# Opening order, bias engine, loops in the overflow path and the decoding rhythm of a fused attention, expert layer and feed-forward kernel

## The chip, the cores and the metric

The kernel runs on one core of a Trainium2 chip. The metric is the time of one execution in microseconds of device time; the median of several executions is compared. The engines are TensorE (PE, with its weight loads as PEld), VectorE (DVE), ScalarE (ACT), GpSimd (POOL) and SyncE (SP, which here issues most transfers). Each runs its own list of instructions in order and waits on semaphores for the others.

## The reference

Three layers follow each other, all in float32. Attention: 2 batches of 8 heads, 576 tokens, 64 wide, with rotary positions on q and k, a softmax over keys, and the product with v. The result is a matrix of 1152 tokens by 512. Expert layer: `logits = x @ w_gate + modality_bias[modality_id]`, each token goes to the expert with the largest logit out of 8, and the output is `gate * (relu(x @ w1[e]) @ w2[e])`, 512 to 1024 to 512. Feed-forward: `h = x @ w_in` (512 to 2048), `g = h * tanh(softplus(h))`, `g @ w_out` (2048 to 512).

With the inputs measured here every batch uses two experts, with 283 to 293 tokens each.

## The kernel before, in words

Products keep float32 accuracy by splitting an operand into a high part (`fp32r`, a rounded copy) and a low part (the rest); a product is then two or three matmuls. So every stage has splits: ACT or POOL write the high part, DVE or POOL subtract to get the low part.

**Attention** (about the first 175 us). For each head, prep loads q and k (`p_load`, `xs`), multiplies by the rotary tables (`p_mul`, L824), adds (`p_add`, L828), makes the high part (`p_hi`, L834) and the low part (`p_lo`, L843) in a buffer `ab` of which there is one, and then four transfers restack it into `sq` and `sk` (`p_stack`, L852 to L855). Scores (L877), maximum (L887), exp (L894), transposes (L907), their splits (L927, L933) and the product with v (L948) follow. Head 0 is prepared by hand in `p_first`, from L789. The order of all other attention work is written by a planner, `Plan`: each operation has an engine, an estimated duration, a key (its rank) and dependencies, and the planner walks a model clock. The estimates are only used to choose the order; the chip then runs it in that order. The planner starts from times at which each engine is supposed to come free (L1008) and from done times of the hand-written part (L1015). Two side jobs are planned too: `setup_dma`, which writes zeros into the padding rows of a scratch tensor in DRAM (two transfers, L277), and `setup_bias`, which makes each token's modality bias (nine small operations on DVE, L286 to L298).

**Expert layer** (to about 312 us). Tokens are sorted by expert in scratch; a tile is 304 rows of one expert. Each batch has two main tiles, (0,0), (0,1), (1,0), (1,1), run by `moe_tile`, with the expert's weights in 8 chunks of 512 KB, each split into high and low by ACT and POOL (L586, L591). An expert with more rows, or a third expert, gives extra tiles. They run in a loop on the device (L1274) between tiles (0,1) and (1,0). Its count is read from memory and is zero for these inputs: the engines come to the loop, meet, and branch past its body. That body is a whole `moe_tile`, written out: by the code 12 transposes, 96 matmuls of the first layer and 96 of the second.

**Feed-forward** (to the end). Weights come as 64-bit words and are decoded by three integer operations per chunk on DVE (`dec`, L1189, L1194, L1199; 16 chunks, 48 operations). Some are done during the expert layer; the rest run beside the feed-forward. There, step q of 32 takes one chunk: q below 16 for the first 640 rows, then again for the other 512. A step has two units `(q, i)`; each has 12 matmuls `h_unit` (L1349), three ACT passes, a DVE reciprocal and a fused multiply (L1371, L1372), a split on ACT and POOL (L1383, L1389), and the matmuls `o_unit` (L1406). The order is a list of events with times in units (`at2`): step q stands at 2q. A unit's matmuls need the PSUM buffer that the DVE multiply of three units before gives back. The weight split of a step, `split_w` (L1332 on ACT, L1333 on POOL), stands at 2q - 1.5. The decoding stands where it must be done in time for that:

```
for z in range(3):
    at2(m - 4.05 + 0.6 * z, lambda n=3 * q + z + 1: decode(n - nd[0]))
```

It is a catch-up: the operation is only issued if fewer than `n` have been.

Of the kernel before, what the change touches and what calls it, by code (L numbers as in the profile page):

```python
# [10 lines left out]
F32 = mybir.dt.float32  # L11
# [3 lines left out]
ALU = mybir.AluOpType  # L15
# [23 lines left out]
P = {'sd': (3,), 'dl': (10, 20), 'qd': (2, 3), 'alt': (0.1, 4), 'd0': 41, 'vl': 9, 'c': (-145.0, 22.5, -2.0), 'w3': 3, 'rq': (0.45, 0.47, 0.2), 'dec': (8, 8, 8), 'rl': 3, 'ah': 0, 'eps': 0.05, 'slack': 0.1}  # L39
# [171 lines left out]
def moe_kernel(ctx: ExitStack, tc: tile.TileContext, aps, out):  # L211
# [63 lines left out]
    def setup_dma():  # L275
        for r0 in (0, T + NTOK):
            nc.sync.dma_start(  # L277
                out=scratch[r0:r0 + T].rearrange("(p a) (h c) -> p (a h) c", p=16, h=2),
                in_=zero[:16, None, :].to_broadcast([16, T // 8, RW // 2]),
            )  # L280

    def setup_bias():
        m = kp.tile([128, B, 5], F32, name="mf")
        sel = kp.tile([128, 2, B, 5], F32, name="msel")
        tmp = kp.tile([128, B, 5, NE], F32, name="mtmp")
        nc.vector.tensor_copy(m, mod[:, :, :, 0])  # L286
        for v in range(2):
            nc.vector.tensor_scalar(
                out=sel[:, v], in0=m, scalar1=float(v), scalar2=None, op0=ALU.is_equal
            )  # L290
        for b in range(B):
            sh = [128, 5, NE]
            for v, o in ((0, lbias), (1, tmp)):
                nc.vector.tensor_tensor(
                    out=o[:, b], in0=sel[:, v, b, :, None].to_broadcast(sh),
                    in1=mbias[:, None, v].to_broadcast(sh), op=ALU.mult,
                )
            nc.vector.tensor_tensor(out=lbias[:, b], in0=lbias[:, b], in1=tmp[:, b], op=ALU.add)  # L298
# [438 lines left out]


    def attention(actx, hook):
# [49 lines left out]
        def p_first():  # L789

            V = nc.vector
            x = xin.pop(0)
            sq = p2.tile([128, S], F32R, tag="sq", name="sq0", bufs=3)
            sk = p2.tile([128, 2, S], F32R, tag="sk", name="sk0", bufs=3)
            for c in (slice(0, NC2), slice(NC2, S)):
                V.tensor_tensor(out=x[:, :, c], in0=x[:, :, c], in1=tabs[:, :, c], op=ALU.mult)
                V.tensor_tensor(out=x[:, 0, c], in0=x[:, 0, c], in1=x[:, 1, c], op=ALU.add)
            q, k = x[0:64, 0], x[64:128, 0]
            nc.scalar.activation(out=sq[0:64], in_=q, func=AF.Copy)
            V.tensor_copy(sk[64:128, 0], k)  # L800
            nc.scalar.activation(out=sk[0:64, 0], in_=k, func=AF.Copy)  # L801
            kh = sk[64:128, 0].bitcast(F32)
            q0, k0 = QT[3][0], 192
            V.tensor_tensor(  # L804
                out=sq[64:128, q0:], in0=q[:, q0:], in1=sq[0:64, q0:].bitcast(F32),
                op=ALU.subtract,
            )
            V.tensor_tensor(out=sk[64:128, 1], in0=k, in1=kh, op=ALU.subtract)
            nc.gpsimd.tensor_tensor(
                out=sk[0:64, 1, :k0], in0=k[:, :k0], in1=kh[:, :k0], op=ALU.subtract  # L810
            )
            V.tensor_tensor(
                out=sk[0:64, 1, k0:], in0=k[:, k0:], in1=kh[:, k0:], op=ALU.subtract
            )
            V.tensor_tensor(
                out=sq[64:128, :q0], in0=q[:, :q0], in1=sq[0:64, :q0].bitcast(F32),
                op=ALU.subtract,
            )
            qk[0] = (sq, sk)
# [3 lines left out]
        def p_mul(n, eng="pool"):  # L823
            lo_eng[eng].tensor_tensor(out=xin[n], in0=xin[n], in1=tabs, op=ALU.mult)  # L824
# [158 lines left out]
        def f_norm(n, hf):  # L983
# [4 lines left out]
            for dst, c0, c1 in (  # L988
# [8 lines left out]
        p_load(0)  # L997
        v_load(0)
        setup_ids()
        p_load(1)  # L1000
        v_load(1)
        setup_mov()
# [3 lines left out]
        p_load(2)  # L1006
        plan = Plan(
            {"pe": 8.9, "act": 8.95, "dve": 10.0, "pool": 8.6, "sp": 7.0},  # L1008
            {"sc": [0.0] * 2, "pexp": [0.0] * 5, "ph": [0.0] * 2, "pha": [0.0], "av": [0.0], "qs": [0.0, 8.6],
             "vhl": [0.0] * 2, "xs": [], "vraw": [], "ab": [0.0], "avt0": [0.0],  # L1010
# [5 lines left out]
             ("vload", 0): ("sp", 5.8), ("vload", 1): ("sp", 8.0), ("vhi", 0): ("act", 8.9)}  # L1016
# [5 lines left out]
        for n in range(B * H):  # L1022
# [6 lines left out]
            if n:  # L1029
# [10 lines left out]
            op("vlo", ("pool", "dve"), (0.82, 0.402), z + pr[5], v_lo, n, deps=[("vhi", n)],  # L1040
               give=[("vraw", n)])
# [55 lines left out]
        plan.op("dma", "sp", 2.0, P["c"][1], setup_dma)  # L1097
        plan.op("bias", "dve", 1.5, P["c"][2], setup_bias)
# [127 lines left out]
    with ExitStack() as mctx:  # L1226
# [312 lines left out]
```

## Time and profile before

| | |
|---|---|
| runs shown | 533.95, 532.73 us, and one of 790.2 us; median 533.95 |
| the profiled execution | 533.38 us, of which 531.7 us are the span from first to last instruction |
| mean granted TensorE clock | 0.968 |
| busy over the span | PE 484.3, PEld 448.2, DVE 412.4, POOL 366.1, ACT 333.0 us |
| moved by DMA | 68.67 MB |

Busy time is an average over stages with different limits, so the stages are read one by one: by windows of time, by the order of instructions in a window, and by who waited for whom. [...]

### The profile page before, as it was taken

What the parts mean: (1) busy time and instruction counts of PE and PEld (TensorE: products, weight loads), DVE (VectorE), ACT (ScalarE), POOL (GpSimd) and SP (SyncE); (2) the same over time, 40 slices, a digit from 0 to 9 for tenths busy, and PEclk for the clock granted to TensorE, in tenths of its full rate; (3) what the DMA queues carried; (4) which work ended last, traced back from release to release, by engine and by line L of the source; (5) the groups of instructions that cost most, each with busy time, mean ns of one, the idle gap of its engine ahead of it and who ended that gap; (6) DMA issues with size and microseconds to landing.
All of it is one profiled execution on the core that took longest, in us unless ns stands there. A gap on an engine that the chain in (4) does not pass through costs nothing. (4 is left out here: it accounts for less than half of the span.)

```text
span 531.7 us, 9169 instructions
## 1 busy us (share of the span) xinstructions
PE 484.3 (91%) x3152; PEld 448.2 (84%) x3152; DVE 412.4 (78%) x629; ACT 333.0 (63%) x747; POOL 366.1 (69%) x350
## 2 busy tenths in 40 slices
PE   1599999998999889997899999999978899999996
PEld 1489999987899788996899988799867788999994
DVE  6958988887898474652367889999999978877773
ACT  2358888865688544545364567766454678777673
POOL 4669999979860537774668766577565668977664
PEclk9869999999999797999799999999999999999999
DMA  8867777866653475594486620002242001100001
GB/s 236 124 187 183 200 182 203 193 176 194 165 108 128 158 273 183 197 310 161 165 293 239 228 90 0 1 0 81 79 159 79 1 2 41 41 21 0 2 1 79
DMA packets 23939, 68.67 MB, mean 129 GB/s; under 512 B 5330, under 2 KB 9618, under 8 KB 21842
## 3 DMA queue, kind: packets, MB, share of 16 engines
q1 hardware_dynamic: 21602, 62.70, 39.9%
q0 software_dynamic: 1456, 4.74, 2.4%
q10 hardware_dynamic: 832, 0.61, 0.4%
q8 instruction: 27, 0.44, 0.3%
q14 instruction: 22, 0.18, 0.1%
HBM read 48.77 MB, written 5.99 MB: 103 GB/s over the span
## 5 line engine op out<-in xcount | busy, mean ns | idle before, releaser
L1371 DVE RECIPROCAL ta<-ta 128x320 f32<-128x320 f32 (+1 forms) x64 | 124.7, 1949 | 21.6 <-ACT ta L1364 20.7
L1389 POOL TENSOR_TENSOR g<-ta,g 128x320 fp32r<-128x320 f32 (+1 forms) x63 | 57.4, 911 | 64.4 <-issue 27.4
L1406 PE MATMUL o<-w2h,g 128*128 128x512 f32 x288 | 100.0, 394 | 0.0
L1333 POOL TENSOR_TENSOR w2l<-wc,w2h 128x512 fp32r<-128x512 f32 x64 | 85.6, 1360 | 3.5 <-ACT w2h L1332 3.5
L1349 PE MATMUL h<-yh,w2h 128*128 128x320 f32 (+1 forms) x256 | 76.4, 298 | 8.5 <-DVE ta L1372 8.5
L1349 PE MATMUL h<-yh,w2l 128*128 128x320 f32 (+1 forms) x256 | 75.9, 296 | 0.6 <-POOL w2l L1333 0.6
L1349 PE MATMUL h<-yl,w2h 128*128 128x320 f32 (+1 forms) x256 | 75.7, 296 | 0.2 <-DVE yl L1297 0.2
L877 PE MATMUL sc<-sk,sq 128*128 128x288 f32 (+1 forms) x320 | 60.2, 321 | 14.1 <-DVE sq L804 9.6
L894 ACT ACTIVATE pexp<-sc,nm 128x576 f32<-128x576 f32 x72 | 53.3, 740 | 28.5 <-DVE nm L887 22.4
L927 ACT ACTIVATE ph<-pt 128x512 fp32r<-128x512 f32 (+2 forms) x112 | 54.7, 509 | 15.6 <-PE pt L907 14.6
L1406 PEld LDWEIGHTS o<-w2h,g 128*128 128x128 f32 x288 | 54.0, 188 | 10.3 <-POOL g L1389 0.3
L887 DVE TENSOR_REDUCE nm<-sc 128x1 f32<-128x576 f32 x72 | 53.5, 752 | 11.4 <-PE sc L877 10.1
L877 PEld LDWEIGHTS sc<-sk,sq 128*128 128x128 f32 (+1 forms) x320 | 48.7, 198 | 15.6 <-ACT sk L801 9.5
L1349 PEld LDWEIGHTS h<-yh,w2h 128*128 128x128 f32 x256 | 48.2, 188 | 13.9 <-issue 8.6
L1406 PE MATMUL o<-w2l,g 128*128 128x512 f32 x144 | 56.7, 394 | 0.0
L907 PE MATMUL pt<-ident,pexp 128*128 128x128 f32 (+1 forms) x360 | 55.1, 282 | 0.7 <-DVE mx L337 0.3
L948 PE MATMUL av<-ph,vhl 128*128 128x256 f32 (+1 forms) x160 | 52.2, 341 | 2.5 <-DVE av L386 0.5
L933 DVE TENSOR_TENSOR pl<-pt,ph 128x512 fp32r<-128x512 f32 (+1 forms) x80 | 49.2, 629 | 4.9 <-ACT ph L927 4.2
L1349 PEld LDWEIGHTS h<-yl,w2h 128*128 128x128 f32 x256 | 48.1, 188 | 2.6 <-DVE yl L1297 0.4
L1383 ACT ACTIVATE g<-ta 128x320 fp32r<-128x320 f32 (+1 forms) x64 | 27.9, 436 | 34.7 <-DVE ta L1372 34.6
L1349 PEld LDWEIGHTS h<-yh,w2l 128*128 128x128 f32 x256 | 48.2, 188 | 0.8 <-POOL w2l L1333 0.8
L907 PEld LDWEIGHTS pt<-ident,pexp 128*128 128x128 f32 (+1 forms) x360 | 43.5, 140 | 2.7 <-PE sc L877 1.1
(446 smaller groups left out, 1241.0 us busy)
## 6 DMA issues: line engine op xcount, KB each, us to landing
wr<-in_wio_dram SPq DMA_DIRECT2D x16, 1024.0 KB, 4.9
xs<-in_qk_dram SPq DMA_DIRECT2D x15, 576.0 KB, 5.3
sk<-ab SPq DMA_DIRECT2D x30, 288.0 KB, 4.0
sq<-ab SPq DMA_DIRECT2D x30, 144.0 KB, 2.3
vraw<-in_v_dram SPq DMA_DIRECT2D x16, 160.0 KB, 2.4
scratch<-zero SPq DMA_DIRECT2D x2, 612.8 KB, 15.7
tabs<-in_rope_dram SPq DMA_DIRECT2D x2, 288.0 KB, 4.6
xs<-in_qk_dram ACTq DMA_DIRECT2D x2, 288.0 KB, 3.9
```

Source lines behind the costliest of these rows:

```text
L877: nc.tensor.matmul(t[:m, hf, :NC2], lhsT=sq[:, c:c + m], rhs=sk[:, z, hf * NC2:(hf + 1) * NC2], start=(z == 0), stop=(z == 1),)
L887: nc.vector.tensor_reduce(out=nm[n, j], in_=sc[n, j][:, :, :NC2], axis=AX.XY, op=ALU.max, negate=True)
L894: nc.scalar.activation(out=pe, in_=sc.pop((n, j))[:, :, :NC2], func=AF.Exp, bias=nm.pop((n, j)), accum_out=st[n, hf][:, i:i + 1],)
L907: nc.tensor.transpose(out=t[:kn, o:o + 128], in_=pexp[n, j][:, k0:k0 + kn], identity=ident)
L927: nc.scalar.activation(out=block(ph, n, hf, kts, slice(0, kn)), in_=psum(n, hf, kts, kn), func=AF.Copy)
L933: nc.vector.tensor_tensor(out=block(pl, n, hf, kts, slice(0, 128)) if kn == 128 else block(ph, n, hf, kts, slice(64, 128)), in0=psum(n, hf ...
L948: nc.tensor.matmul(av[n, hf][:, :u.nq], lhsT=vhl[n][:, kt].rearrange("p a d -> p (a d)"), rhs=src[:, kt, u.at:u.at + u.nq], start=(kt == 0 ...
L1333: nc.gpsimd.tensor_tensor(out=lo[:, cs], in0=w[:, cs], in1=hi[:, cs].bitcast(F32), op=ALU.subtract)
L1349: nc.tensor.matmul(ps[:, :w], lhsT=wt[:, c], rhs=m[g, i][:, c], start=(n == 0), stop=(n == 11))
L1371: nc.vector.reciprocal(out=ta, in_=ta)
L1389: eng.tensor_tensor(out=gt[q][1][:, o:o + w], in0=tas.pop((q, i))[:, :w], in1=gt[q][0][:, o:o + w].bitcast(F32), op=ALU.subtract,)
L1406: nc.tensor.matmul(acc[g, t], lhsT=a[:, s], rhs=b, start=(f == 0 and z == 0), stop=(f == FC2 - 1 and z == 2),)
```

## The change

Six edits. (1) Loads of the opening are reordered: q and k of head 1 come before v of head 0, those of head 2 before the gate weights and the modality. (2) In `p_first` the split of q is cut in a late part (columns 320 on, used by the first scores) and an early part, the piece that POOL did goes to DVE, and `v_lo` of head 0 is placed on DVE right behind it. Head 1's `p_mul` is cut into four instructions. (3) The two zero transfers become 14, each with six of 38 pieces per partition, planned on SP behind the restacking of heads 3 to 7. (4) `setup_bias` moves from DVE (key -2) to POOL (key 60). (5) The extra tile's body becomes `extra_tile`, with two loops on the device inside it. (6) In the feed-forward one or two decode operations per step, from step 1 to 15, are issued beside the catch-up.

```diff
-    def setup_dma():
-        for r0 in (0, T + NTOK):
-            nc.sync.dma_start(
-                out=scratch[r0:r0 + T].rearrange("(p a) (h c) -> p (a h) c", p=16, h=2),
-                in_=zero[:16, None, :].to_broadcast([16, T // 8, RW // 2]),
-            )
+    def setup_dma(i):
+        r0, i = (T + NTOK) * (i % 2), i // 2
+        a = slice(6 * i, min(6 * i + 6, T // 8))
+        nc.sync.dma_start(
+            out=scratch[r0:r0 + T].rearrange("(p a) (h c) -> p (a h) c", p=16, h=2)[:, a],
+            in_=zero[:16, None, :].to_broadcast([16, a.stop - a.start, RW // 2]),
+        )
...
-        nc.vector.tensor_copy(m, mod[:, :, :, 0])
+        nc.gpsimd.tensor_copy(m, mod[:, :, :, 0])
...
+    def extra_tile(r):
...
+        with tc.For_i(0, FC1 // 2) as i:
+            hi, lo = chunk(i)
+            for j in range(2):
...
+                ps = products(wh, wl, xh, xl, KC)
...
+        with tc.For_i(0, KC) as d:
+            wh, wl = (w.rearrange("p (c d) -> p c d", c=FC1) for w in chunk(d + FC1 // 2))
+            ps = products(wh, wl, hh, hl, FC1)
...
+            nc.scalar.activation(out=qh[:, late], in_=q[:, late], func=AF.Copy)
+            V.tensor_copy(kh, k)
+            nc.scalar.activation(out=sk[top, 0], in_=k, func=AF.Copy)
+            q_lo(late)
+            for r in (low, top):
+                V.tensor_tensor(out=sk[r, 1], in0=k, in1=kh.bitcast(F32), op=ALU.subtract)
+            nc.scalar.activation(out=qh[:, early], in_=q[:, early], func=AF.Copy)
+            q_lo(early)
...
         def p_mul(n, eng="pool"):
-            lo_eng[eng].tensor_tensor(out=xin[n], in0=xin[n], in1=tabs, op=ALU.mult)
+            x = xin[n]
+            for c in (slice(0, NC2), slice(NC2, S)) if n == 1 else (slice(0, S),):
+                for z in (slice(0, 1), slice(1, 2)) if n == 1 else (slice(0, 2),):
...
         p_load(0)
+        p_load(1)
         v_load(0)
+        v_load(1)
+        p_load(2)
+        setup_mov()
         setup_ids()
-        p_load(1)
-        v_load(1)
-        setup_mov()
         setup_consts()
         p_first()
         v_hi(0, "act")
-        p_load(2)
+        v_lo(0, "dve")
         plan = Plan(
-            {"pe": 8.9, "act": 8.95, "dve": 10.0, "pool": 8.6, "sp": 7.0},
+            {"pe": 9.6, "act": 11.0, "dve": 11.8, "pool": 10.0, "sp": 7.0},
...
-        plan.op("dma", "sp", 2.0, P["c"][1], setup_dma)
-        plan.op("bias", "dve", 1.5, P["c"][2], setup_bias)
+        for i in range(14):
+            op("zero", "sp", 0.5, 20.0 + 5.0 * i, setup_dma, i, deps=[("stack", 3 + i // 3)])
+        op("bias", "pool", 2.5, 60.0, setup_bias)
...
-            regs["x"] = tile_regs(row)
-            fx = Feed(["x"])
-            for _ in moe_tile("x", fx, bank3):
-                pass
+            extra_tile(tile_regs(row))
...
+            if 0 < q < FC2:
+                for z in range(1 + q % 2):
+                    at2(m + 0.6 + z, decode, 1)
```

`products` issues three matmuls for each of its column blocks: 12 in each of the two calls of the first loop's body, 24 in the second's. With the 12 transposes the body of the extra tile then has 60 matmuls and transposes in its code.

## Rows read from the trace of the kernel before

**Rows 1.** Windows: PE, PEld, DVE, ACT, POOL busy (instructions), PEclk, DMA share, GB/s.
```profile
75.00:100.00 25.00, 25.00 (x205) 24.65 (x204) 22.18 (x51) 20.89 (x51) 23.69 (x26) 1.00 0.77 195
```
**Rows 2.** Timeline, opening: start, length, engine, line, operation; in brackets idle before.
```profile
17.17 3.41 SPq L853 DMA_DIRECT2D sq<-ab  x1
...
18.41 2.65 DVE L294 TENSOR_TENSOR lbias<-msel,mbias 128x40 f32<-128x40 f32 x1
...
22.45 1.41 DVE L887 TENSOR_REDUCE nm<-sc 128x1 f32<-128x576 f32 x2
...
23.62 0.60 SPq L855 DMA_DIRECT2D sk<-ab  x1
...
27.94 3.23 PE L877 MATMUL sc<-sk,sq 128*128 128x288 f32 x12
28.00 0.67 POOL L834 TENSOR_SCALAR ab<-xs 128x576 fp32r<-128x576 f32 x1 [5.21 <-DMA sk<-ab]
```
**Rows 3.** The page's DMA issues: count, KB each, median us to landing.
```profile
sk<-ab SPq DMA_DIRECT2D x30, 288.0 KB, 4.0
...
scratch<-zero SPq DMA_DIRECT2D x2, 612.8 KB, 15.7
```
**Rows 4.** Timeline, a small POOL operation.
```profile
50.41 0.23 POOL L966 TENSOR_SCALAR rs<-stt 128x3 f32<-128x3 f32 x1
```
**Rows 5.** Windows of the opening, columns as in rows 1.
```profile
24.00:36.00 12.00, 10.26 (x42) 9.52 (x43) 6.16 (x14) 5.35 (x14) 5.37 (x5) 0.50 0.91 232
...
38.00:50.00 12.00, 12.00 (x98) 11.64 (x97) 10.94 (x23) 10.25 (x25) 11.43 (x13) 1.00 0.65 162
```
**Rows 6.** One line's instructions, the loop L1274: count, ns min/median/max, first and last start.
```profile
L1274 PEldq COMPARE_BRANCH  x3: 97/192/3301, 246.5 to 253.9; - x3
```
**Rows 7.** Timeline around the loop.
```profile
248.78 0.30 PE L682 MATMUL mm<-hh(0, 1)_3117,wlo(0, 1)_7_3326 128*128 128x304 f32 x1
...
250.27 0.35 SPq L578 DMA_DIRECT2D wraw(1, 0)_3_3807<-in_w_dram  x1
...
252.14 2.34 POOL L591 TENSOR_TENSOR wlo(1, 0)_1_3803<-wraw(1, 0)_1_3322,whi(1, 0)_1_3801 128x1024 fp32r<-128x1024 f32 x1 [6.05 <-ACT whi(1, 0)_1_3801 L586]
254.18 0.29 PEld L682 LDWEIGHTS mm<-xh(1, 0)_3355,whi(1, 0)_0_3383 128*128 128x128 f32 x1 [5.35 <-issue]
```
**Rows 8.** The page: busy time and instructions by engine; the queue of code: packets, MB, share.
```profile
PE 484.3 (91%) x3152; PEld 448.2 (84%) x3152; DVE 412.4 (78%) x629; ACT 333.0 (63%) x747; POOL 366.1 (69%) x350
...
q8 instruction: 27, 0.44, 0.3%
```
**Rows 9.** The same queue in 249.5 to 254.2 us.
```profile
q8 instruction: 2, 0.03, 2.9%
```
**Rows 10.** Windows behind the loop, columns as in rows 1.
```profile
254.00:260.00 6.00, 5.82 (x27) 5.82 (x28) 0.47 (x1) 0.60 (x2) 2.83 (x2) 0.61 0.55 175
260.00:266.00 6.00, 6.00 (x45) 6.00 (x44) 3.65 (x6) 3.41 (x6) 4.29 (x2) 1.00 0.51 175
```
**Rows 11.** Groups by line, DVE, 316.6 to 423.0 us: busy, mean ns, idle before.
```profile
L1371 DVE RECIPROCAL ta<-ta 128x320 f32<-128x320 f32 x28 | 60.1, 2145 | 2.3 <-ACT ta L1364 2.3
...
L1194 DVE SCALAR_TENSOR_TENSOR wc<-wr,wc 128x1024 int32<-128x1024 int32 x7 | 9.6, 1367 | 0.0
L1189 DVE TENSOR_SCALAR wc<-wr 128x1024 int32<-128x1024 int32 x7 | 8.9, 1275 | 0.0
L1199 DVE SCALAR_TENSOR_TENSOR wc<-wr,wc 128x1024 int32<-128x1024 int32 x7 | 8.5, 1218 | 0.0
```
**Rows 12.** The decoding's lines over the whole run, as rows 6.
```profile
L1189 DVE TENSOR_SCALAR wc<-wr x16: 682/1376/3348, 201.5 to 411.6; 128x1024 int32<-128x1024 int32 x16
L1194 DVE SCALAR_TENSOR_TENSOR wc<-wr,wc x16: 1214/1218/2416, 204.9 to 415.5; 128x1024 int32<-128x1024 int32 x16
```
**Rows 13.** Timeline: one POOL weight split and a decode operation in it.
```profile
360.66 2.55 POOL L1333 TENSOR_TENSOR w2l<-wc,w2h 128x512 fp32r<-128x512 f32 x2
362.03 2.27 DVE L1194 SCALAR_TENSOR_TENSOR wc<-wr,wc 128x1024 int32<-128x1024 int32 x1
```

More of the change, by code (lines that the diff above doesn't have):

```diff
@@ L293, in setup_bias @@
             for v, o in ((0, lbias), (1, tmp)):
-                nc.vector.tensor_tensor(
+                nc.gpsimd.tensor_tensor(
                     out=o[:, b], in0=sel[:, v, b, :, None].to_broadcast(sh),
@@ L297, in setup_bias @@
                 )
-            nc.vector.tensor_tensor(out=lbias[:, b], in0=lbias[:, b], in1=tmp[:, b], op=ALU.add)
+            nc.gpsimd.tensor_tensor(out=lbias[:, b], in0=lbias[:, b], in1=tmp[:, b], op=ALU.add)
     regs = {}
@@ L736, in moe_tile, with chunk, products @@
                 yield from moe_x(nxt, bank)
+    def extra_tile(r):
+        regs["x"] = r
+        load_rows("x")
+        for _ in moe_x("x", cur["bank"]):
+            pass
+        xh, xl = xsplit.pop("x")
+        hh = mp.tile([128, FC1, T], F32R, tag="hh", name="hhx")
+        hl = mp.tile([128, FC1, T], F32R, tag="hl", name="hlx")
+        yc = r["y"]()
+        def chunk(i):
+            pool = wpool[-1]
+            w = pool.tile([128, 1024], F32, tag="wraw", name="wrawx")
+            nc.sync.dma_start(
+                out=w, in_=aps["w12"][ds(r["e"] * NCH + i, 1)].rearrange("o p c -> (o p) c")
+            )
+            hi = pool.tile([128, 1024], F32R, tag="whi", name="whix", bufs=1)
+            nc.scalar.activation(out=hi, in_=w, func=AF.Copy)
+            lo = pool.tile([128, 1024], F32R, tag="wlo", name="wlox", bufs=1)
+            nc.vector.tensor_tensor(out=lo, in0=w, in1=hi.bitcast(F32), op=ALU.subtract)
+            return hi, lo
+        def products(hi, lo, mh, ml, n):
+            ps = cur["bank"]()
+            for c in range(n):
+                for z, (w, m) in enumerate(((hi, mh), (hi, ml), (lo, mh))):
+                    nc.tensor.matmul(
+                        ps[:, :T], lhsT=w[:, c], rhs=m[:, c], start=(c == 0 and z == 0),
+                        stop=(c == n - 1 and z == 2),
+                    )
+            return ps
+        with tc.For_i(0, FC1 // 2) as i:
+            hi, lo = chunk(i)
+            for j in range(2):
+                wh, wl = (
+                    w.rearrange("p (c f) -> p c f", c=KC)[:, :, j * 128:(j + 1) * 128]
+                    for w in (hi, lo)
+                )
+                ps = products(wh, wl, xh, xl, KC)
+                h = hh[:, ds(2 * i + j, 1)].rearrange("p o t -> p (o t)")
+                nc.scalar.activation(out=h, in_=ps[:, :T], func=AF.Relu)
+                nc.vector.scalar_tensor_tensor(
+                    out=hl[:, ds(2 * i + j, 1)].rearrange("p o t -> p (o t)"),
+                    in0=ps[:, :T], scalar=0.0,
+                    in1=hh[:, ds(2 * i + j, 1)].rearrange("p o t -> p (o t)").bitcast(F32),
+                    op0=ALU.max, op1=ALU.subtract,
+                )
+        with tc.For_i(0, KC) as d:
+            wh, wl = (w.rearrange("p (c d) -> p c d", c=FC1) for w in chunk(d + FC1 // 2))
+            ps = products(wh, wl, hh, hl, FC1)
+            nc.scalar.activation(
+                out=Y[:, ds(d, 1), ds(yc, T)].rearrange("p o t -> p (o t)"),
+                in_=ps[:, :T], func=AF.Copy,
+            )
@@ L798, in p_first, with q_lo @@
             q, k = x[0:64, 0], x[64:128, 0]
[L799 to L818, printed above, removed]
+            q0 = QT[3][0]
+            late, early, top, low = slice(q0, S), slice(0, q0), slice(0, 64), slice(64, 128)
+            qh, kh = sq[top], sk[low, 0]
+            def q_lo(c):
+                V.tensor_tensor(
+                    out=sq[low, c], in0=q[:, c], in1=qh[:, c].bitcast(F32), op=ALU.subtract
+                )
+            nc.scalar.activation(out=qh[:, late], in_=q[:, late], func=AF.Copy)
[6 more added lines that the diff above has]
+            q_lo(early)
             qk[0] = (sq, sk)
@@ L1039, in attention @@
                    take=[("vhl", n)])
-            op("vlo", ("pool", "dve"), (0.82, 0.402), z + pr[5], v_lo, n, deps=[("vhi", n)],
-               give=[("vraw", n)])
+            if n:
+                op("vlo", ("pool", "dve"), (0.82, 0.402), z + pr[5], v_lo, n, deps=[("vhi", n)],
+                   give=[("vraw", n)])
         tiles, groups, was, e_was = 0, 0, (), ()
```

11 lines of the change are left out of this document (7 added, 4 removed).

## The prediction

> **What bounds the kernel now.** I read first the windows by stage, then the timeline of the stages in which PE waits, then the lines of the engine that it waits for.
>
> Once attention runs, it is PE's: in 75 to 100 us PE is busy all 25.00 us and POOL 23.69 [rows 1]. So a microsecond that PE loses before that is lost for good, as long as POOL, which prepares the heads, keeps up. Three places have slack that this change can touch.
>
> The first is the opening. Head 1's scores begin on PE at 27.94 and POOL goes on with head 2 at 28.00, after 5.21 us of idling, both when the last restacking transfer of head 1 has landed [rows 2]. That transfer is issued by L855 at 23.62 [rows 2] and such a one lands after 4.0 us [rows 3]. It was issued so late because the ones before it on SP's queue were slow: L853 begins at 17.17 and takes 3.41 us only to be issued, where L855, the last, takes 0.60 [rows 2]. In front of them in the queue stand the two zero transfers, 612.8 KB each, 15.7 us to landing [rows 3]. On DVE, meanwhile, a maximum that the scores have long been ready for starts only at 22.45, behind the bias operations, one of which (128x40) takes 2.65 us [rows 2]. And in 24 to 36 us the granted clock is 0.50, with 42 matmuls in 12 us, against 98 in the 12 us from 38 on at 1.00 [rows 5].
>
> The second is the loop over extra tiles. PE's last matmul before it ends at 249.08 and its next weight load comes at 254.18; SP is past the loop by 250.27 [rows 7]. One branch of PE there takes 3301 ns, against a median of 192 [rows 6]. In this gap, and in it alone, two packets of code come in on queue q8 within 5 us [rows 9], of 27 in the whole run [rows 8]. From 254 to 260 the mean clock is 0.61 [rows 10].
>
> The third is the first half of the feed-forward. From the first reciprocal to the 28th, DVE is idle for 2.3 us out of 106.4; the 21 decode operations in it take 9.6, 8.9 and 8.5 us [rows 11]. So DVE is full there, not only late in it.
>
> **The change, part by part.** The sum is made against the profiled execution's 533.38 us (span 531.7 and 1.7 around it); the median of the runs, 533.95, is 0.6 above it.
>
> Zeros, loads and head 1: the zero transfers leave the queue in front of the restacking. L853 waits for POOL's last operation on head 1 and is ready at 17.17 already [rows 2]. Cutting `p_mul` into four lets DVE's subtractions in between, so I put POOL's end 0.5 later (a quarter of L294's 2.65, which is the length of one such wait), though the earlier load may give that back. Then L853 is issued at 17.7, and L855, two issues of 0.6 behind it at its own pace, at 18.9 [rows 2]; it lands 4.0 later [rows 3], at 22.9: 5.0 before 27.94. Bounds: 3, if the reordered loads of heads 1 and 2 are still in the queue, and 6.3. I take 5.0, as the chain of row durations gives it.
>
> The clock: from 27.94 to 36 PE works at 0.50. If it had 1.00, half of these 8 us would go, 4.0 at most; if the clock drops again as in [rows 5], nothing. PE's gap before head 1 gets shorter but does not go away, so I take 1.5, between a third and a half, and keep 0 and 4.0.
>
> Bias: its nine operations go to POOL, at 9 x 0.23 = 2.1 us by the smallest POOL operation that the rows show [rows 4]. They run among the prep of heads 5 to 8, where POOL has 1.3 us of room in 25 [rows 1]; queued behind them is the prep of one head, and PE waits for that only if it comes late. POOL itself gets its 5.0 us earlier start too, and its 5.21 us wait is gone, so the cover is there; without it the cost is 2.1. DVE's gain (the maximum at 22.45) stands beside the wait for the transfers, which ends later, and is not counted again.
>
> The 14 zero transfers cost SP 14 issues of about 0.6, in a queue that is not full, and transfer time: two of them land within 15.7 us of issue [rows 3], so one of 14 is at most 2 x 15.7 / 14 = 2.2 us of the queue and about 1.1 if they shared it. The DMA share is 0.77 there [rows 1]: three parts per head of some 8.5 us take it close to full. Loads then land later; their slack hides it, and without the slack one head waits for up to 3 parts, 3.4 us. I take 0 for both. Opening in all: 6.5 us, between 1 and 10.
>
> The loop: PE's body by the code falls from 204 to 60 matmuls and transposes, each with a weight load. A q8 packet is 0.44 MB / 27 = 16.3 KB [rows 8]; over PE's 3152 matmuls and as many loads that is at least 230 instructions, some 115 pairs. The old body spans nearly two packets, so its end is not among the code that PE holds and two are fetched [rows 9]. The new one is about half a packet and ends in the packet being read or the next. PE's branch should then cost what its median does, 0.19 [rows 6]: PE starts at 250.27 + 0.2 = 250.5, and after a gap of 1.4 us instead of 5.1 I expect no fall of the clock. 45 matmuls take 6.00 us at full clock, 0.133 each [rows 10]. The 24 of the first chunk end at 253.7; the next chunk's low part is ready at 252.14 + 2.34 = 254.5 [rows 7], so PE waits 0.8. The 27 that before are done by 260 [rows 10] are then done by 254.9. The gain is 5.1; I take 5.0. Bounds: 0 (the fetch stays) and 5.5. [...]
>
> Decoding: the same 21 operations stay in this stretch, the last ones at step 13 instead of 15. DVE was full, so at most the 2.3 idle us go [rows 11], and what the operations wait. Undisturbed the three take 0.68 and 1.21 and 1.21 us or so [rows 12] (L1199 has L1194's form), 21.7 for seven of each, against 27.0 now: 5.3 is waiting. The waits show in one pair: POOL's two splits run from 360.66 to 363.21, and the decode begun at 362.03 takes 2.27, ending 1.1 after POOL [rows 13]. Dealt operations stand right behind a reciprocal, as POOL's splits for the coming step run; I allow 0.4 us for each of 13 steps, 5.2, and so no change in waits. Of the idle time 1.0 goes. Gain 1.0, between 7.6 (no idling, no waits) and a loss of 30 (all 21 at the longest, 7 x 3.35 + 14 x 2.42 = 57.3, less 27.0).
>
> The rest, loads reordered and subtractions regrouped in `p_first`, moves first scores by a microsecond or two, in time that ends at the transfers anyway: nothing.
>
> Sum: 6.5 + 5.0 + 1.0 = 12.5; 533.4 - 12.5 = 520.9, say **521 us**.
>
> **Rivals.** *A, the opening's gain is given back.* Bias on POOL, zeros among the loads, and a new planned order hold up prep in a stretch where POOL has only 1.3 us of room in 25 [rows 1]. Against it: PE waits for no prep there now. At 2.1 + 3.4 us it leaves 1.0 of the 6.5: 526.4. *B, the jump still fetches code*, because the new body crosses into a packet that is not there, or the other engines' barrier is the limit. For it: only before's single case is known. 533.4 - 6.5 - 1.0 = 526. *C, the clock does not fall in the opening*: 2.5 more, 518, and down to 515 with fewer decode waits. *D, slower: the dealt decoding meets POOL.* DVE is full from start to end [rows 11], and a decode operation and a POOL split keep each other out [rows 13]. Now the late catch-up makes ACT's split wait for the decoding, so POOL runs behind it; when chunks are decoded ahead, POOL's two splits move to just where the dealt operation stands. If each of the 21 waits for one POOL instruction of 1.25 us (half of 2.55) more than now, that is 26 us: 533.4 - 11.5 + 26 = 548. It decides from 0.55 us per operation on (11.5 / 21). Against it: undisturbed decodes are the median in the run's L1194 [rows 12]. [...] *E, the loops inside the skipped body, or the new order, do nothing and only the noise of the plan is left*: 531.
>
> **How the numbers follow.** Forecast 0.50, with its own range of 517.5 to 524.5; A 0.16, B 0.12, C 0.14, D 0.05, E 0.03. 2% of the median is 10.7 us, so faster by over 2% (what a measurement of this kernel can tell from no change) means under 523.3. The forecast lies under it in about three of four cases (0.38), C always (0.14), A and B in one of ten (0.03): 0.55. Slower by over 2% is most of D, 0.03. The rest, 0.42, is within 2%. The range of 514 to 528 takes in forecast, C, and most of A and B, and leaves out D, E and the far bounds, some 0.15.
>
> **What would show it.** Opening: L855 of head 1 issued by 19 and PE's scores of head 1 by 23; if they come at 27 or 28, that step is wrong. Attention: PE at 25 of 25 us from 50 to 100 with no wait for `sq` or `sk`; waits there mean A. Loop: no branch of PE over 1 us, no pair of q8 packets, PE's gap under 2 us, clock 1.00 behind it. Feed-forward: the stretch from the first to the 28th reciprocal 105 or so instead of 106.4; 21 decodes near 27 us in sum, over 38 means D. A total over 528 would say that the order of attention, which the planner writes anew, costs what I put at nothing.

## The result, and the profile after

The changed kernel takes 524.81 us (median of 523.95, 524.09, 525.53 and 526.75) against 533.64 for the kernel before: ratio 0.9845, 95% interval 0.9805 to 0.9885. That is 1.6% faster, under the 2% line but clear of zero. The profiled execution has 523.95 us and a span of 522.2, 9.5 less than before. Forecast: 521, range 514 to 528.

The page of the changed kernel: busy time by engine, the queue of code, and DMA issues (count, KB each, median us to landing), to set against [rows 8] and [rows 3].

```profile
PE 479.5 (92%) x3152; PEld 442.8 (85%) x3152; DVE 408.6 (78%) x621; ACT 332.8 (64%) x748; POOL 368.7 (71%) x360
...
q8 instruction: 26, 0.43, 0.3%
...
sk<-ab SPq DMA_DIRECT2D x30, 288.0 KB, 3.8
...
scratch<-zero SPq DMA_DIRECT2D x12, 96.8 KB, 4.4
```

PE has the same instructions; a code packet is gone; the zeros come in small parts (12 of the 14 are in the records).

The opening, as [rows 2]: timeline, start and length in us, in brackets the idle time before.

```profile
17.45 0.53 SPq L914 DMA_DIRECT2D sq<-ab  x1
17.45 0.76 DVE L949 TENSOR_REDUCE nm<-sc 128x1 f32<-128x576 f32 x1 [0.57 <-PE sc L939]
...
18.94 0.50 SPq L915 DMA_DIRECT2D sq<-ab  x1
...
20.14 0.60 SPq L917 DMA_DIRECT2D sk<-ab  x1
...
24.25 3.16 PE L939 MATMUL sc<-sk,sq 128*128 128x288 f32 x12 [0.78 <-DMA sk<-ab]
24.28 0.68 POOL L896 TENSOR_SCALAR ab<-xs 128x576 fp32r<-128x576 f32 x1 [1.06 <-DMA sk<-ab]
```

The second restacking transfer (L915, formerly L853) takes 0.50 us to issue instead of 3.41; the last one (L917) goes out at 20.14 instead of 23.62; PE's scores of head 1 begin at 24.25 instead of 27.94. The maximum that stood behind the bias until 22.45 is done from 17.45 on.

The windows that answer to [rows 5] and [rows 1] (PE, PEld, DVE, ACT, POOL busy with instructions; granted clock; DMA share; GB/s):

```profile
24.00:36.00 12.00, 10.91 (x72) 10.16 (x73) 8.23 (x15) 8.24 (x21) 9.71 (x12) 0.87 0.77 215
75.00:100.00 25.00, 24.48 (x198) 23.77 (x197) 22.35 (x49) 20.45 (x51) 23.46 (x29) 1.00 0.69 174
```

From 24 to 36 us PE now runs 72 matmuls at a mean clock of 0.87, before 42 at 0.50. From 75 to 100 us it is busy for 24.48 us, before for all 25.00.

Around the loop: its branch on PE (count, ns min/median/max), the timeline, the code packets in 243.5 to 246 us, and the window behind it, as [rows 6, 7, 9, 10].

```profile
L1339 PEldq COMPARE_BRANCH  x3: 97/187/310, 240.9 to 245.4; - x3
```
```profile
243.17 0.30 PE L684 MATMUL mm<-hh(0, 1)_3132,wlo(0, 1)_7_3341 128*128 128x304 f32 x1
...
245.61 0.62 PE L684 MATMUL mm<-xh(1, 0)_3370,whi(1, 0)_0_3398 128*128 128x304 f32 x1 [2.14 <-issue]
```
```profile
q8 instruction: 1, 0.02, 2.3%
```
```profile
245.50:251.50 6.00, 5.89 (x31) 5.89 (x32) 1.10 (x3) 3.03 (x5) 4.74 (x2) 0.72 0.53 171
```

The longest branch fell from 3301 to 310 ns and PE's gap, start to start of the two matmuls, from 5.40 to 2.44 us. One packet of code still comes in inside the gap, and the clock behind it is still only 0.72.

What is left of the gap is behind the long branch. PE's queue has twelve semaphore instructions there, by which the engines meet, and a second branch. The kernel before in 252.61 to 254.3 us, then the changed kernel in 243.98 to 245.6 (count, ns min/median/max, first and last start):

```profile
L1274 PEldq EVENT_SEMAPHORE  x12: 51/51/51, 252.7 to 253.8; - x12
```
```profile
L1339 PEldq EVENT_SEMAPHORE  x12: 51/51/51, 244.0 to 245.3; - x12
```

From the end of the long branch to the first matmul it is 1.58 us before (252.60 to 254.18) and 1.64 after (243.97 to 245.61). Of the two packets before, the first comes in during the long branch (249.30 to 252.60), the second among the semaphore instructions (252.66 to 254.2); the one packet of the changed kernel comes in among them too (244.03 to 245.6), and none during its branch. Each of these instructions takes 51 ns all the same. So the shorter branch, 2.99 us, makes the whole of the 2.96 that the gap lost, and the packet that is left is not seen to hold PE up.

The feed-forward, the groups of DVE that answer to [rows 11], 307.9 to 411.9 us (busy, mean ns, idle before):

```profile
L1433 DVE RECIPROCAL ta<-ta 128x320 f32<-128x320 f32 x28 | 60.0, 2144 | 0.6 <-ACT ta L1426 0.6
L1264 DVE SCALAR_TENSOR_TENSOR wc<-wr,wc 128x1024 int32<-128x1024 int32 x7 | 12.1, 1733 | 0.0
L1259 DVE SCALAR_TENSOR_TENSOR wc<-wr,wc 128x1024 int32<-128x1024 int32 x7 | 9.3, 1331 | 0.0
L1254 DVE TENSOR_SCALAR wc<-wr 128x1024 int32<-128x1024 int32 x7 | 5.5, 779 | 0.0
```

The 21 operations take 26.9 us in all, before 27.0. The wait has only changed places: the first operation of a chunk went from 1275 to 779 ns, the third (L1264, formerly L1199) from 1218 to 1733.

A ledger of the profiled executions, cut at places that every kernel passes (starts of instructions, in us). "Loop" is from the last matmul before the loop to the first reciprocal of the feed-forward, so it holds main tiles (1,0) and (1,1) as well as the gap; "feed-forward" is from the first to the 64th and last reciprocal. The rows below the second are the experiments that follow. All columns but the last are of one execution each, and executions differ: of the six runs of changed_again, two lie at 523.1 and 523.3 us, the profiled one among them, and four at 526.4 to 527.9. The kernels were run in four groups, each with the kernel before beside it (medians 533.64, 533.38, 533.76 and 534.20), so times of different groups are compared by their ratios to it.

| kernel | last matmul before the loop | PE's gap at the loop | loop | feed-forward | median of runs |
|---|---|---|---|---|---|
| before | 248.78 | 5.40 | 67.91 | 204.24 | 533.64 |
| changed | 243.17 | 2.44 | 64.77 | 203.56 | 524.81 |
| open_only | 241.91 | 5.70 | 67.83 | 204.25 | 526.64 |
| zeros_bias | 243.56 | 5.52 | 67.69 | 204.26 | 526.92 |
| zeros_only | 250.12 | 5.42 | 67.96 | 204.24 | 532.96 |
| bias_only | 255.69 | 5.43 | 68.39 | 204.22 | 536.71 |
| loop_only | 249.54 | 2.44 | 64.72 | 204.23 | 530.90 |
| deal_only | 249.75 | 5.84 | 68.16 | 203.57 | 533.44 |
| bare_loop | 249.19 | 1.03 | 64.86 | 203.48 | 530.10 |
| no_loop | 248.85 | 0.14 | 62.66 | 203.56 | 524.68 |
| changed_again | 242.68 | 2.41 | 64.57 | 203.59 | 526.99 |
| open_loop | 243.77 | 2.44 | 64.41 | 204.23 | 524.82 |
| deal_shifted | 243.62 | 2.44 | 66.57 | 203.08 | 523.14 |
| mul_uncut | 242.55 | 2.44 | 66.29 | 204.84 | 526.01 |

For the change: 5.61 before the loop, 3.14 in it and 0.68 in the feed-forward make 9.43 us.

### The profile page after: what moved, and what is told of

Its sections match the earlier page's. It is cut to its first block, busy times and chain, and to the rows that moved or that the text cites. A ratio compares the mean times of both kernels' runs of the same rounds, so it can differ in the third digit from the quotient of the medians.

```text
span 522.2 us, 9180 instructions
## 1 busy us (share of the span) xinstructions
PE 479.5 (92%) x3152; PEld 442.8 (85%) x3152; DVE 408.6 (78%) x621; ACT 332.8 (64%) x748; POOL 368.7 (71%) x360
## 4 chain that ended last, share of the span: by engine, by line
PE 33%; DVE 13%; DMA 2%; issue 2%; ACT 2%; POOL 0%; POOLq 0%; SPq 0%; ACTq 0%
PE h L1411 15%; PE o L1468 14%; DVE ta L1433 5%; PE mm L684 4%; DVE yl L1359 2%; DVE wc L1264 2%; DVE wc L1259 2%; DMA wraw(1, 1)_6_4051<-in_w_dram 1%; DMA wraw(1, 1)_3_3940<-in_w_dram 1%; DVE ta L1434 1%; DVE wc L1254 1%; POOL out_dram L1478 0%; DVE xl(1, 1)_3879 L657 0%; POOLq L1600 0%; ACT w2h L1394 0%
## 5 line engine op out<-in xcount | busy, mean ns | idle before, releaser
L1451 POOL TENSOR_TENSOR g<-ta,g 128x320 fp32r<-128x320 f32 (+1 forms) x63 | 60.1, 954 | 61.4 <-issue 29.0
L1445 ACT ACTIVATE g<-ta 128x320 fp32r<-128x320 f32 (+1 forms) x64 | 27.9, 436 | 41.4 <-DVE ta L1434 41.4
```

The source lines that it names most:

```text
L1451: eng.tensor_tensor(out=gt[q][1][:, o:o + w], in0=tas.pop((q, i))[:, :w], in1=gt[q][0][:, o:o + w].bitcast(F32), op=ALU.subtract,)
```

## The experiments

The theory after the result was that the three parts add up: opening 5.6, loop 3.4, decoding 0.6. The rivals were that a part shows only together with another, and for the opening that the order of loads and not the zeros carried it. The first four kernels are the kernel before with parts of the change.

**open_only**: all edits of the attention part (load order, `p_first`, the cut `p_mul`, the 14 zero transfers, `setup_bias` on POOL, the planner's start times); extra tile and decoding as before.

> The kernel before with all four edits of the attention part (load order, p_first, the 14 zero transfers, bias on POOL) and without the loops and the dealt decoding. Theory 1, the gains add up and the opening is worth what the two traces show at the last Y before the loop, 5.6 us (249.12 to 243.51): about 5.6 faster than before, 528.1; the last restacking transfer of head 1 issued near 20.1, PE's scores of head 1 near 24.3, and behind the loop the same 5.1 us gap as before. Theory 2, part of it only shows because a later stage is faster too: 3 us or less, over 530.


Measured: ratio 0.9876 (0.9849 to 0.9902), median 526.64 beside 533.38. The last restacking transfer of head 1 goes out at 20.36, its scores start at 24.49, the gap at the loop is still 5.70. Theory 1, a little above its 5.6.

**loop_only**:

```diff
+    def extra_tile(r):
...
-            regs["x"] = tile_regs(row)
-            fx = Feed(["x"])
-            for _ in moe_tile("x", fx, bank3):
-                pass
+            extra_tile(tile_regs(row))
```


> The kernel before with the body of the extra tile as loops and nothing else. Theory 1, the shorter jump saves one of two code packets and the clock falls less: 3.4 us as between the two traces (5.6 to 9.0 between the last Y before the loop and hh 8), 530.3; PE's gap 2.4 instead of 5.1, one packet of code in it. Theory 2, the gain behind the loop comes from the opening's shift of other engines against PE: under 1 us, over 532.6, and PE's gap near 5.


Measured: 0.9952 (0.9930 to 0.9973), 530.90. In 249.5 to 252.0 us, with the idle time of PE ahead of its first matmul:

```profile
q8 instruction: 1, 0.02, 2.8%
```
```profile
251.98 0.41 PE L682 MATMUL mm<-xh(1, 0)_3355,whi(1, 0)_0_3383 128*128 128x304 f32 x1 [2.14 <-issue]
```

The gap is 2.44 with one packet, to the hundredth what it is in the changed kernel: the loop's gain is its own. The packet that is saved is the one in the branch: with the old body the branch takes 3281 to 3701 ns and a packet comes in during it, in all six traces; with the new body it takes 310 ns and none does, in all six. From the last matmul before it to the first product with hh it saves 3.40 us (20.84 to 17.44), to the first reciprocal 3.19.

**deal_only**:

```diff
+            if 0 < q < FC2:
+                for z in range(1 + q % 2):
+                    at2(m + 0.6 + z, decode, 1)
```


> The kernel before with only the dealt decoding. Theory 1, the stretch to the 29th reciprocal gets 2.4 us shorter and 1.7 is given back at step 13, where catch-up and dealt operations come together: 0.6 faster in all, 533, with the first to the 29th reciprocal about 104 instead of 106.4. Theory 2, the shortening belongs to the other edits (clock and loads at the start of the feed-forward): 0, or up to 1.5 slower, since the three decodes at step 13 stay; the same stretch 106 or more.


Measured: 0.9990 (0.9970 to 1.0009). The runs cannot tell it from nothing. The trace can: first to 29th reciprocal 104.1, first to last 203.57 against 204.24. Theory 1, and a term of 0.7. By the ratios the three parts alone make 1.2, 0.5 and 0.1%, 1.8% in all, and the whole change 1.6% (1.4% in changed_again below); with intervals of 0.2 to 0.4% either way, no run shows that a part needs the others.

**zeros_bias**: zeros and bias alone, loads and `p_first` as before.

```diff
  setup_dma(i) and setup_bias as in the change
...
-        plan.op("dma", "sp", 2.0, P["c"][1], setup_dma)
-        plan.op("bias", "dve", 1.5, P["c"][2], setup_bias)
+        for i in range(14):
+            op("zero", "sp", 0.5, 20.0 + 5.0 * i, setup_dma, i, deps=[("stack", 3 + i // 3)])
+        op("bias", "pool", 2.5, 60.0, setup_bias)
```


> The kernel before with the 14 zero transfers and the bias on POOL alone; loads and p_first as before. Theory 1, the opening's gain is the zeros leaving the queue in front of the restacking: at least 3.7 of the 5.6 us, 530 or less, with PE's scores of head 1 at 24 or 25 instead of 27.94. Theory 2, the order of loads and of p_first carries it (head 1's q and k come earlier): 1 us or less, 532.5 or more, PE's scores of head 1 at 27 or later.


Measured: 0.9865 (0.9834 to 0.9896), 526.92. That is all of open_only's gain, with no new load order and no new `p_first`. Theory 1, but the next two kernels show that its wording, "the zeros leaving the queue", is only half of it.

**zeros_only** and **bias_only**: one of the two each.

```diff
 zeros_only, setup_dma(i) as in the change
...
-        plan.op("dma", "sp", 2.0, P["c"][1], setup_dma)
+        for i in range(14):
+            op("zero", "sp", 0.5, 20.0 + 5.0 * i, setup_dma, i, deps=[("stack", 3 + i // 3)])
 bias_only, setup_bias as in the change
...
-        plan.op("bias", "dve", 1.5, P["c"][2], setup_bias)
+        plan.op("bias", "pool", 2.5, 60.0, setup_bias)
```


> The kernel before with the 14 zero transfers and nothing else; the bias stays on DVE in its old place. Theory 1, the whole gain of zeros_bias (6.5 us) is SP's queue and the DMA engines freed in front of head 1's restacking: 527 to 528, the second restacking transfer of head 1 taking about 0.5 us to issue instead of 3.41. Theory 2, the bias operations on DVE, which hold a maximum until 22.45, are an equal cause: only half of it, 530, since the product with v of head 0 still starts at 24 to 25.

> The kernel before with the bias on POOL (key 60) and nothing else; the two whole zero transfers stay where they were. Theory 1: PE then does head 0's product with v some 4 us earlier but waits for head 1's scores until 27 to 28 all the same, so 0 to 1 us, 532.5 to 533.5. Theory 2: half of the 6.5 us, 530.


Measured: zeros_only 0.9945 (0.9905 to 0.9985), bias_only 1.0046 (1.0019 to 1.0074). One alone gives 0.55% or costs 0.46%; both together give 1.35%. The openings say why. In the kernel before, PE does not wait for the transfers at all. It waits for DVE, ahead of the product with v of head 0:

```profile
24.51 0.58 PE L948 MATMUL av<-pl,vhl 128*128 128x256 f32 x1 [4.61 <-DVE pl L933]
```

From there it has one further wait, 0.47 us for ACT ahead of 27.06, until it comes to the scores of head 1 at 27.94, just when the last transfer has landed (POOL goes on at 28.00) [rows 2]. Timeline of zeros_only, and two of its windows:

```profile
18.02 0.50 SPq L855 DMA_DIRECT2D sq<-ab  x1
...
19.22 0.59 SPq L857 DMA_DIRECT2D sk<-ab  x1
...
19.26 2.65 DVE L296 TENSOR_TENSOR lbias<-msel,mbias 128x40 f32<-128x40 f32 x1
...
23.31 1.41 DVE L889 TENSOR_REDUCE nm<-sc 128x1 f32<-128x576 f32 x2
...
25.37 0.58 PE L950 MATMUL av<-pl,vhl 128*128 128x256 f32 x1 [4.54 <-DVE pl L935]
...
28.79 2.97 PE L879 MATMUL sc<-sk,sq 128*128 128x288 f32 x12
```
```profile
24.00:30.00 6.00, 4.16 (x17) 3.83 (x18) 3.00 (x7) 2.68 (x7) 2.23 (x3) 0.54 0.44 139
30.00:36.00 6.00, 4.99 (x34) 4.46 (x33) 4.11 (x10) 3.65 (x10) 2.90 (x2) 0.89 0.75 200
```

The transfers are out 4.4 us earlier, but PE does not take the scores of head 1: they stand behind the product with v of head 0, which waits 4.54 us for a split on DVE, and that stands behind the bias operations in DVE's order. After that wait the clock is 0.54, and the scores start at 28.79, later than before. Timeline of bias_only, and the first of these windows:

```profile
17.29 3.55 SPq L853 DMA_DIRECT2D sq<-ab  x1
...
22.18 0.66 PE L978 MATMUL xo<-mov,avt 128*128 128x72 f32 x4 [0.47 <-ACT avt L957]
...
24.07 0.59 SPq L855 DMA_DIRECT2D sk<-ab  x1
...
28.43 3.22 PE L877 MATMUL sc<-sk,sq 128*128 128x288 f32 x12 [5.59 <-DMA sk<-ab]
```
```profile
24.00:30.00 6.00, 1.57 (x6) 1.56 (x7) 0.00 (x0) 0.00 (x0) 1.35 (x2) 0.52 0.88 251
```

Here PE is through with head 0 by 22.8 and then waits 5.59 us for the transfers, and the clock falls as well. In zeros_bias neither wait is left:

```profile
25.50 0.67 PE L980 MATMUL xo<-mov,avt 128*128 128x72 f32 x4 [0.47 <-ACT avt L959]
25.97 1.83 PE L879 MATMUL sc<-sk,sq 128*128 128x288 f32 x12
```
```profile
24.00:30.00 6.00, 4.35 (x31) 3.87 (x31) 3.37 (x9) 2.34 (x7) 3.83 (x7) 1.00 0.79 225
```

The clock stays at 1.00 and twelve score matmuls take 1.83 us instead of 3.22. So these were two waits of nearly the same end, one behind the other in PE's order, and with either left the clock fell (0.54 and 0.52 in 24 to 30 us). Theory 2 of zeros_only was right that the bias is an equal cause, but the two do not add. It is not so in every execution: three of the ten runs of zeros_only lie at 527.4 to 528.5 us, the others, the profiled one (534.77) among them, at 531.4 to 535.0; what differs in those three was not seen. Why bias_only ends 2.5 us slower is not settled; its trace, of the slowest of its ten runs (540.78; the others 535.2 to 538.4), is level with the kernel before at 116 us and 6.9 us late at the loop, in the order that the planner wrote anew.

**bare_loop** and **no_loop**: the changed kernel with the loop's body cut to a row load, and without the loop. Extra tiles are left out in both; with these inputs there are none.

```diff
 bare_loop
-            extra_tile(tile_regs(row))
 no_loop
-        with tc.For_i(0, n_extra) as it:
-            row = lp.tile([1, 2], I32, tag="xr", name="xr")
-            nc.sync.dma_start(out=row, in_=extra[ds(it, 1), :])
-            extra_tile(tile_regs(row))
```


> The changed kernel with the loop over extra tiles kept, but its body cut to the load of one row number (extra tiles are not computed; there are none with these inputs). Theory 1, what remains of PE's gap (2.4 us) and the clock fall behind it is the fetch of the one code packet that the 60 pairs still need: PE's gap about 1.2 us or less, no packet or only the next in line, clock 1.00 behind it, 2 us faster than the changed kernel, 522 to 523. Theory 2, the rest is the meeting of the engines (13 waits of 51 ns and two branches on PE's queue): the gap stays near 2.2, and 524.5 like the changed kernel.

> The changed kernel without the loop over extra tiles at all (they are not computed; there are none with these inputs). Both theories: no gap of PE between the last Y of the tile before and the first matmul of the next but that for data, clock 1.00 there; 3 us faster than the changed kernel, about 521.5. If it is no faster than bare_loop by over 0.5 us, a loop with a small body costs next to nothing (theory 1); if the meeting of the engines is the cost (theory 2), nearly all 3 us show only here.


Measured: 530.10 (0.9908, 0.9868 to 0.9948) and 524.68 (0.9809, 0.9763 to 0.9854). Neither is shown to be faster than the changed kernel; as whole times both expectations failed. At the loop bare_loop's numbers look like theory 1: no code packet lies in 249.2 to 250.3, and PE:

```profile
250.22 0.41 PE L684 MATMUL mm<-xh(1, 0)_3370,whi(1, 0)_0_3398 128*128 128x304 f32 x1 [0.73 <-ACT Y L734]
```
```profile
250.20:256.20 6.00, 5.55 (x38) 5.31 (x39) 3.56 (x4) 3.69 (x5) 4.11 (x2) 1.00 0.37 119
```

Two packets, one, none: gaps of 5.40, 2.44 and 1.03 us, and clocks behind it of 0.61, 0.72 and 1.00. But bare_loop took more away than the packet. PE's queue passes the branch and all but the end of the meeting there while PE is still at the matmuls before:

```profile
L1339 PEldq EVENT_SEMAPHORE  x12: 51/51/986, 247.3 to 248.6; - x12
```

The last of those matmuls starts at 249.19. In the changed kernel the same twelve instructions come behind the last matmul and fill 1.3 of the 2.44 us. And in no_loop a packet comes in as well, in 248.8 to 249.3, where PE has no gap (0.14). So bare_loop does not part the two theories; the rows of the changed kernel speak for theory 2. The sign that was named for theory 2, a gain in no_loop alone, came in (62.66 against 64.86), but bare_loop lost its gain only at the next border. The 2.3 us that bare_loop is ahead at the first product with hh (15.19 after the last matmul, changed kernel 17.45) are gone at the first reciprocal: 64.86 against 64.77. There PE waits 2.62 us for DVE's split of Y, where it waits 1.13 in the changed kernel, and the window from 309 on shows the clock falling:

```profile
311.97 0.42 PE L1410 MATMUL h<-yl,w2h 128*128 128x320 f32 x1 [2.62 <-DVE yl L1358]
```
```profile
309.00:315.00 6.00, 3.38 (x16) 3.12 (x15) 5.35 (x4) 2.62 (x6) 3.62 (x3) 0.80 0.48 175
```

At that border DVE's split is the limit in bare_loop. It is not always so: no_loop is 3.4 us ahead at the first product with hh (14.09), waits 1.14, and keeps 2.1 us at the first reciprocal; the last section says what differs. The other loss is not explained: bare_loop reaches the loop at 249.19 and no_loop at 248.85, the changed kernel at 243.17 and 242.68, although the instructions up to there stand in the same order. In both traces PE has a wait of 2.1 us at 120 us for an evacuation on ACT that the changed kernel does not have, and from 120 to 125 bare_loop's clock is 0.66. no_loop is within 0.2 us of the changed kernel from the 5th to the 50th maximum, and 1.7 late from the 51st, at 120 us. Why ACT is late there stays open. no_loop's profiled run, 527.51, is the slowest of its five (the others 524.1 to 525.2), so its loss before the loop need not stand for them; bare_loop's, 530.0, is one of five at 529.4 to 530.7.

**changed_again, open_loop, deal_shifted, mul_uncut**, run side by side. changed_again is the changed kernel; open_loop leaves out the dealing (the three lines of deal_only); the others:

```diff
 deal_shifted
-                for z in range(1 + q % 2):
+                two = q % 2 or q in (10, 12)
+                for z in (0, 1) if two else (1,):
                     at2(m + 0.6 + z, decode, 1)
 mul_uncut
-            for c in (slice(0, NC2), slice(NC2, S)) if n == 1 else (slice(0, S),):
...
+            lo_eng[eng].tensor_tensor(out=xin[n], in0=xin[n], in1=tabs, op=ALU.mult)
```


> The changed kernel itself, as the measure for the others of this group on the same chip. Expected 524.8 again, between 524 and 527; the stretch before 250 us can differ by 2 or 3 from one execution to another.

> The changed kernel without the dealt decoding: catch-up alone, as before. Theory 1, dealing is worth 0.7 from the first to the last reciprocal, as deal_only's trace shows (203.57 against 204.24): 0.4 to 1.0 slower than the changed kernel, and the first to the 29th reciprocal back to 106.4 from 104.0. Theory 2, dealing is only worth something when the rest is faster: 2 us slower.

> The changed kernel with the dealt operations of the even steps moved from 0.6 to 1.6 behind the step's start, and one more operation in steps 10 and 12, so that step 13 issues one instead of three. Theory 1, the third operation of a chunk takes 1.73 us instead of 1.22 because it meets POOL's weight split, and step 13 gives back 1.7: the third operation near 1.3 us, no stall of PE at step 13, the first to the last reciprocal 201 to 202 instead of 203.6, the whole 2 us faster than the changed kernel. Theory 2, the wait for POOL moves to another operation or to POOL's own splits, which come late for PE: no gain, first to last reciprocal 203 or more.

> The changed kernel with head 1's rotary product as one POOL instruction again instead of four; the planner writes its order with the same estimates. Theory 1, the cut costs POOL time (4.20 us for the four, 2.64 for the one before) and delays head 1: restacking issued up to 1.5 earlier than 20.1, the opening up to 1 us shorter. Theory 2, the one long instruction holds up DVE's splits of head 0 at 10 to 13 us instead, as in zeros_bias (first scores at 16.0 instead of 12.7): head 1 as early, but the first maximum later than 13.7, and no gain or a loss of 1.


Measured: changed_again 0.9864 (0.9829 to 0.9899), open_loop 0.9840 (0.9812 to 0.9869), deal_shifted 0.9804 (0.9762 to 0.9845), mul_uncut 0.9858 (0.9819 to 0.9896). These intervals overlap, so no order among the four is shown. By the stretches, open_loop loses the 0.64 us that theory 1 gave (204.23 against 203.59), too little for the runs to see. mul_uncut, dealt as well, has 204.84; it is 1.3 us behind the changed kernel by the fifth reciprocal already.

In deal_shifted, DVE's groups from 310.1 to 416.6 us:

```profile
L1264 DVE SCALAR_TENSOR_TENSOR wc<-wr,wc 128x1024 int32<-128x1024 int32 x7 | 9.7, 1392 | 0.0
L1259 DVE SCALAR_TENSOR_TENSOR wc<-wr,wc 128x1024 int32<-128x1024 int32 x7 | 9.3, 1330 | 0.0
L1254 DVE TENSOR_SCALAR wc<-wr 128x1024 int32<-128x1024 int32 x7 | 8.9, 1276 | 0.0
```

The third operation is cured, 1392 ns, and the first has the wait again, 1276. The sum is 27.9, not less. Theory 2 for the waits. The stall at step 13 is gone as theory 1 had it (PE waits 1.78 us at 409.06 in the changed kernel, at most 0.40 here), and the feed-forward is 0.5 shorter, 203.08, not 2. It has the lowest median of all, 523.14; that it beats the changed kernel is not shown.

mul_uncut gives one for the other. The changed kernel first, then mul_uncut:

```profile
9.52 2.02 DVE L873 TENSOR_TENSOR sk<-xs,sk 64x576 fp32r<-64x576 f32 x2
9.99 4.20 POOL L884 TENSOR_TENSOR xs<-xs,tabs 128x288 f32<-128x288 f32 x4 [6.34 <-DMA xs<-in_qk_dram]
```
```profile
9.34 3.92 DVE L873 TENSOR_TENSOR sk<-xs,sk 64x576 fp32r<-64x576 f32 x2
10.03 2.61 POOL L881 TENSOR_TENSOR xs<-xs,tabs 128x1152 f32<-128x1152 f32 x1 [6.37 <-DMA xs<-in_qk_dram]
```

Uncut, POOL saves 1.6 and DVE's two subtractions take 1.9 longer; the last restacking goes out at 18.63 instead of 20.14, the first maximum comes at 15.39 instead of 13.68, and head 1's scores start at 24.98, later than 24.18 in changed_again. Each theory had one half.

## Why the prediction came out as it did

Each of the three places gave a gain, and the sum was 3.1 too large: 12.5 forecast, 9.4 in the profile (by the medians 8.8, and 7.2 in changed_again). That it would be faster by over 2% had 0.55; it came out at 1.6%. What bounds PE was misread in two of the places.

**Opening, 6.5 forecast, 5.6 measured, 6.1 in changed_again.** The split between its terms was off. Transfers: 3.7 instead of 5.0. The step that failed is "I put POOL's end 0.5 later". L915 is ready at 18.94, not 17.7, since the cut product took 4.20 us and not 2.64, and the high part of head 1 took 1.66 us, before 0.67, beside a product that the planner gave to DVE. From there the chain held: two issues later 20.14, landing 4.1 us behind that. The clock: 1.5 was low, as far as a difference can say. The 21st maximum starts at 57.28 and 56.20 in the two traces of the changed kernel, before at 62.66; less the 3.7 of the scores that leaves 1.7 and 2.7. In changed_again the clock never leaves 1.00 from 18 to 36 us, as rival C had it; in the first trace it falls for a short time (0.74 in 24 to 30 us). That DVE's gain "stands beside the wait for the transfers, which ends later", was a misreading. In the trace before, PE waits 4.61 us for DVE and none for the transfers, and the two end within 0.1 us of each other. With the transfers alone, as in zeros_only's trace, their 4.4 us come to nothing, since the bias stays on DVE. That the sum of this part came near is luck to that extent: it counted one of two waits, and the change removes both.

**Rival A** did not come in: the lead is 5.4 us at the 21st maximum and 5.6 at the loop. **Load order and `p_first`**, put at nothing: open_only and zeros_bias agree within 0.3 us.

**Loop, 5.0 forecast, 3.1 to 3.4 measured.** This term made most of the error. The step that failed is PE "starts at 250.27 + 0.2": it lets PE go on a branch after SP, but behind its long branch PE still has the twelve semaphore instructions and the second branch, 1.6 us, in both kernels. PE was idle for 2.14 us and not 1.4. The step before it held: the new body "ends in the packet being read or the next", no packet came in during the branch, and the branch took 310 ns (0.19 us forecast). The clock behind the gap, forecast at 1.00, was 0.72; with the same gap of 2.44 it was 1.00 in deal_shifted and mul_uncut, and what decides is not shown. Of rival B the fetch did not come in; its other ground, "the other engines' barrier", is what is left of the gap. How much of its code PE holds was the author's estimate, and no run shows it; what the runs show is one packet in the long branch before (3301 ns) and none in the branch of the changed kernel (310 ns).

**Decoding, 1.0 forecast, 0.7 measured.** DVE's idle time fell more than said, from 2.3 to 0.6 us where 1.0 was to go, and the 29th reciprocal came 2.3 us earlier; the waits stayed (26.9 against 27.0 us), so D is out. What the text did not see is step 13, where catch-up and dealt operations issue three in a row and PE waits 1.78 us, so that 0.7 is left at the last reciprocal. Over the whole stretch PE's waits for DVE's multiply fell from 8.5 us to 6.2.

## What to carry to other kernels

When two engines keep PE waiting until nearly the same moment, removing either may give nothing and removing both everything (here 0.55% faster and 0.46% slower alone, 1.35% faster together); so a part that does nothing alone is tried with the other before it is dropped. A skipped loop on the device cost twice here: the branch, when code came in during it (3.30 us against 0.31), and the meeting of the engines behind it, 1.6 us, which a shorter body left as it was. A sum for such a gap goes through the waiting engine's own queue, instruction by instruction, and not only to the moment at which another engine is past it. And where DVE is full and POOL works beside it, moving operations moved the wait to another one (27.0, 26.9 and 27.9 us for the 21 operations).

## What the runs showed that was not expected

Time won before a border was lost at it, by which of DVE and POOL began first (3.08 us against 0.88 for the same two splits). In deal_shifted and mul_uncut the gap at the loop is 2.44 as in the changed kernel, but the clock stays at 1.00 behind it, so that the first product with hh comes 1.5 us earlier. At the start of the feed-forward PE then waits 2.98 and 2.97 us for the split of Y, the clock falls there to 0.79 in both, and the stretch is 1.5 to 1.8 us longer than in the changed kernel (66.57 and 66.29 against 64.77). In deal_shifted:

```profile
307.78 0.64 PE L1411 MATMUL h<-yl,w2h 128*128 128x320 f32 x1 [2.98 <-DVE yl L1359]
```
```profile
303.60:309.60 6.00, 3.02 (x16) 2.77 (x15) 5.60 (x5) 2.92 (x7) 4.77 (x3) 0.79 0.34 120
```

A clock that stays up does not cost this by itself: in no_loop it is at 1.00 behind the loop too, and the loop stretch is the shortest, 62.66. What differs is a pair of DVE's splits of Y. First the changed kernel, then deal_shifted with POOL's weight split:

```profile
301.21 0.88 DVE L1359 TENSOR_TENSOR yl<-Y,yh 128x320 fp32r<-128x320 f32 x2
```
```profile
302.04 3.08 DVE L1359 TENSOR_TENSOR yl<-Y,yh 128x320 fp32r<-128x320 f32 x2
```
```profile
301.92 2.85 POOL L1395 TENSOR_TENSOR w2l<-wc,w2h 128x512 fp32r<-128x512 f32 x2 [2.70 <-ACT w2h L1394]
```

In deal_shifted POOL begins 0.12 us before the pair, which then takes 3.08 us instead of 0.88; in the changed kernel POOL begins at 301.72, half a microsecond after it. In mul_uncut the pair takes 3.08 us as well, in bare_loop 1.99, in no_loop 0.88. That is 2.2 us of DVE's time just ahead of the split that PE waits for; the clock, which falls behind PE's wait (0.64 in 309.6 to 315.6 us of deal_shifted, where the changed kernel has 1.00 from 309.2 to 315.2), adds to the loss, and how much is not separated.
